# A new instruction order for linear attention and a spatial gating layer: q decayed in natural layout, powers of lambda formed by GpSimd

## The chip, the cores and the metric

One Trainium2 chip, one of its cores. Five engines take part, each with a queue of its own that it works off in order: TensorE (PE, with its weight loads as PEld), VectorE (DVE), ScalarE (ACT), GpSimd (POOL) and SyncE (SP). Sixteen DMA engines move data between HBM and the on-chip memory SBUF, and two kinds of queue feed them here: SP's loads, stores and transposes, and GpSimd's transfers, which also turn float32 into bfloat16 on the way. The metric is the time of one execution in microseconds, the median of the runs.

## The reference

Two layers follow each other. q, k and v have 4 batches, 8 heads, 768 positions and 64 channels, and each head has a decay `lam` near 0.98. The first layer is linear attention in blocks of 64 positions:

```python
rel = pos[:, None] - pos[None, :]
Dmask = np.where(rel >= 0, lam[:, None, None] ** rel[None, :, :], 0.0)
...
for b in range(nb):
    intra = (q_b @ k_b.T * Dmask) @ v_b
    inter = (q_b * lam ** (pos + 1)) @ kv_state
    out_b = intra + inter
    kv_state = lam ** 64 * kv_state + (k_b * lam ** (63 - pos)).T @ v_b
```

The second is a gated layer on x, which is that output with the heads side by side (4 x 768 x 512):

```python
h = np.maximum(x @ w_in, 0.0)              # 512 -> 1024
u, v = h[..., :512], h[..., 512:]
v_n = (v - mean(v)) / sqrt(var(v) + 1e-6)
v_s = w_spatial @ v_n + b_spatial          # over the 768 positions
out = (u * v_s) @ w_out                    # 512 -> 512
```

## The kernel before, in words

The decay between two positions is a product of two powers, `lam ** (MID - j)` for a key at j and `lam ** (i - MID)` for a query at i, so the mask that is left holds only zeros and ones. The work is cut into 12 steps, 3 to a batch, each of 256 positions (128 partitions, two neighbouring positions to a partition, 8 heads).

One string, `ORDER`, holds the whole program, each word one operation as `NAME.arguments.ENGINE`, with T for TensorE, D, A, P and S for the others. `KM.5.1.P` is "decay the second half of k of step 5, on GpSimd". An engine gets its words in the order of the string, and waits between engines come from the tiles that an operation reads and writes. What the words are:

- LQ, LK, LV: SP's loads of q, k and v of a step, 512 KB each, three buffers for each. VC casts v to bfloat16.
- KM: k times its power of lambda, to bfloat16, in natural layout (positions on the partitions); QM is the same for q, and QC casts q without decay.
- TK, TQ: transposes on TensorE, eight 128x128 ones for a step; EK, EQ bring them out of PSUM into kT and qT. Where q came by QC, EQ multiplies by `lq`, the powers in transposed layout. DK, DQ: the transposes by DMA in place of these, issued by SP; for them q has to come by QM.
- SC: scores; MK: the mask of zeros and ones, out of PSUM; KV: the state, KS: scores and state interleaved, SS: copy of the state to SBUF; AV: the output of attention, transposed; EX brings it out as xT. SC, KV, KS and AV are made of matmuls of 64x64 weights, four of which lie side by side in the array; TensorE's other operations use 128x128.
- PV, EV: the v half of `x @ w_in` and its relu; BN, RA, RD, NB, VN: mean, variance, root, reciprocal, shift and the normalised vn. PU, EU: the u half, transposed, and its relu.
- WI, WS, WO: GpSimd's transfers of w_in (two halves, the v half first), w_spatial (two halves of rows) and w_out. BS: SP's load of b_spatial, repeated on all partitions. WT, EW: w_spatial transposed, once.
- GP, PW, GM: for a batch, eight groups: bias into PSUM, the spatial matmul (L514, 6 of 384 columns), the product with u. PW of a batch needs all six vn tiles of that batch.
- PO, EO, ST: the last matmul, its copy, its store; PH, EH, SH the same in halves of the columns.
- FL: four 128x128 matmuls whose result nobody reads; FN: a copy of one element that nobody reads, ahead of EX; GT: a GpSimd copy of one element that holds GpSimd until a load is there.

The preparation of the powers is in `c_lam` to `l_t`: lambda is brought to all partitions by a matmul, ACT takes the logarithm, DVE multiplies by the positions, and ACT takes exponentials, of 128x48 elements for the natural layout and of 128x256 elements twelve times for `lq`. Steps 0 to 4 use QC and TQ with `lq`; steps 5 to 11 use QM, DK and DQ.

PSUM has eight banks; the last arguments of many words are bank numbers, and bank 7 holds the attention state.

Of the kernel before, what the change touches and what calls it, by code (L numbers as in the profile page):

```python
# [8 lines left out]
FP32 = mybir.dt.float32  # L9
# [10 lines left out]
TK.1.1.3.T TK.1.0.2.T KV.0.0.T EQ.1.0.0.D TQ.1.1.1.T MK.0.1.5.6.D EK.1.0.2.D SS.0.0.A EK.1.1.3.A VC.1.P  # L20
SC.1.0.4.5.T LQ.2.S QC.2.0.D SC.0.0.2.3.T LK.2.S EQ.1.1.1.D KV.0.1.T GT.1.1.P QC.2.1.P WI.1.P SC.1.1.0.1.T
FL.4.6.T MK.0.0.2.3.D TQ.2.0.2.T MK.1.1.0.1.D AV.0.0.3.6.T FN.0.3.6.A TQ.2.1.0.T SS.0.1.A MK.1.0.4.5.D LT.2.A
KM.2.0.P KV.1.0.T AV.1.0.1.4.T KM.2.1.D WS.1.P TK.2.0.5.T AV.0.1.3.6.T LV.2.S SS.1.0.D FN.1.1.4.A KV.1.1.T
LK.3.S EX.0.1.6.A AV.1.1.1.4.T BS.S LK.5.S EX.1.0.1.A EK.2.0.5.D LQ.3.S EX.0.0.3.D PV.0.1.5.T FL.15.6.T
EX.1.1.4.A WO.P TK.2.1.3.T GT.1.2.P PV.1.1.1.T EV.1.1.1.A EQ.2.1.0.D EQ.2.0.2.D VC.2.P WT.0.0.0.T EK.2.1.3.D
SC.2.0.2.3.T PV.1.0.4.T BN.1.1.D PV.0.0.6.T EW.0.0.0.A MK.2.0.2.3.D EV.0.1.5.A EV.1.0.4.A SC.2.1.0.1.T SS.1.1.A
PU.1.1.5.T BN.1.0.D WT.2.0.4.T KV.2.0.T MK.2.1.0.1.D RA.1.A BN.0.1.D LV.3.S AV.2.0.2.3.T EV.0.0.6.D SS.2.0.A
FN.2.2.3.D PU.1.0.0.T BN.0.0.D AV.2.1.2.3.T EX.2.1.3.D RD.1.D WT.1.0.1.T RA.0.A NB.1.D RD.0.D EX.2.0.2.A
EW.1.0.1.D EW.2.0.4.A NB.0.D VN.0.0.A WT.1.1.6.T GT.2.1.P KM.3.0.P EW.1.1.6.D KM.3.1.P GT.2.2.P VC.3.P
WT.2.1.3.T EW.2.1.3.D PV.2.1.2.T PV.2.0.1.T VN.1.0.A PU.2.1.4.T EU.1.0.0.A VN.0.1.D LK.4.S LQ.4.S KM.4.1.P  # L30
KM.4.0.P EV.2.0.1.A QC.4.2.P PU.0.0.6.T LV.4.S PU.0.1.3.T LQ.5.S WT.0.1.0.T LV.5.S LK.6.S VN.1.1.A PU.2.0.1.T
EU.1.1.5.A EV.2.1.2.D BN.2.1.D BN.2.0.D RA.2.A RD.2.D EU.0.0.6.A GP.0.2.1.2.A EW.0.1.0.D VN.2.1.D GP.0.0.0.5.A
VN.2.0.D EU.0.1.3.A QC.3.2.D LQ.6.S GP.0.1.1.6.A EU.2.0.1.D TK.3.2.0.T PW.0.0.0.5.T GM.0.0.0.5.D EU.2.1.4.D
GP.0.2.0.3.A PW.0.2.0.3.T TQ.3.2.1.T EQ.3.2.1.D GM.0.2.0.3.D EK.3.2.0.A PW.0.2.1.2.T SC.3.1.4.5.T MK.3.1.4.5.D
KS.3.0.0.1.T SS.3.0.A GP.0.0.1.3.A PW.0.1.1.6.T GP.0.3.1.4.A KS.3.1.0.1.T KM.5.1.P KM.5.0.P DK.5.S GM.0.2.1.2.D
MK.3.0.0.1.D TK.4.2.5.T EK.4.2.5.A PW.0.0.1.3.T PW.0.3.1.4.T GP.0.1.0.2.A GM.0.1.1.6.D GP.0.3.0.0.D AV.3.0.1.5.T
GM.0.0.1.3.D TQ.4.2.6.T SS.3.1.A PW.0.3.0.0.T GM.0.3.1.4.D PW.0.1.0.2.T FN.3.1.5.D AV.3.1.1.5.T EX.3.0.1.A
VC.4.P EQ.4.2.6.D KS.4.0.3.4.T SS.4.0.A PO.0.5.6.T EO.0.5.6.A QM.5.1.P KS.4.1.3.4.T VC.5.P QM.5.0.D SS.4.1.A
# [36 lines left out]
EO.2.3.6.D RD.11.D NB.11.D VN.11.1.A VN.9.1.D GP.3.3.1.4.D PU.10.0.0.T VN.11.0.D PO.2.2.2.T VN.10.0.A EO.2.2.2.A
PU.11.1.6.T GP.3.0.1.1.D PW.3.0.1.1.T EU.10.1.5.D EU.10.0.0.D GM.3.0.1.1.D GP.3.2.0.2.A EU.11.1.6.A PW.3.2.0.2.T
PW.3.3.1.4.T ST.2.1.S GP.3.2.1.5.A GP.3.1.1.0.D PW.3.0.0.3.T PW.3.1.1.0.T PW.3.2.1.5.T GP.3.3.0.6.D ST.2.5.S
GM.3.3.1.4.D GM.3.2.1.5.D ST.2.2.S GP.3.1.0.1.A GM.3.1.1.0.D PW.3.1.0.1.T PW.3.3.0.6.T GM.3.1.0.1.D PO.3.4.4.T
# [7 lines left out]
def kernel(  # L86
# [37 lines left out]
    ps = psum.tile([P, 8, 512], FP32, name="ps")  # L124
    SB = 7

    lam_in = sb([1, H], FP32, "lam_in")
    one_row = sb([1, P], FP32, "one_row")
    loglam = sb([P, H], FP32, "loglam")
    llrow = sb([P, 4], FP32, "llrow")  # L130
# [457 lines left out]
```

## Time and profile before

| what | value |
|---|---|
| time, median of 2 runs | 147.72 us (147.72 to 147.73) |
| profiled execution, span from first to last instruction | 145.4 us (what lies outside the span isn't in the profile) |
| mean granted TensorE clock | 0.996 |
| busy: PE, PEld, DVE, ACT, POOL | 131.9, 83.2, 113.0, 76.2, 53.7 us |
| DMA | 32.28 MB, mean 222 GB/s |
| read from HBM, written | 24.77 MB, 6.29 MB |

How to read what is quoted from it. The page gives busy times and, as digits, the busy tenths of 40 equal slices of the span. Groups of instructions stand as `line engine op out<-in shapes xcount | busy us, mean ns of one | idle before, and what ended it`. The timeline gives `start us, us, engine, line`, and in brackets how long the engine had been idle and what released it. The chain of waits gives `start us, us, what` for the chain that ended last; on TensorE its pieces follow each other without a gap, so the length of a piece is what that work costs in the queue, while the mean of a matmul in the groups is its latency. The windows give, for a stretch A:B, its length and each engine's busy time, with the granted clock, the DMA share and GB/s at the end.

### The profile page before, as it was taken

To read this page: it belongs to the slowest core of one execution; us is meant where nothing else is said; L and a number is where in the kernel's file an instruction comes from. 1 tells how busy PE (TensorE), PEld (TensorE's weight loads), DVE (VectorE), ACT (ScalarE), POOL (GpSimd) and SP (SyncE) were. 2 spreads that over 40 slices of the span, in tenths; PEclk is the share of its full clock that TensorE was granted. 3 is DMA by queue.
4 is the path that set the end of the run, shared out by engine and by line. 5 is a ranking of instruction groups with operands and counts; after the bars stand their busy time and mean duration, and the time that the engine had idled before them with its cause. 6 is when DMAs were issued, how large, how long until landed. Compare 5 with 4: busy or idle time off the path is not lost.

```text
span 145.4 us, 4626 instructions
## 1 busy us (share of the span) xinstructions
PE 131.9 (91%) x1954; PEld 83.2 (57%) x1954; DVE 113.0 (78%) x229; ACT 76.2 (52%) x155; POOL 53.7 (37%) x66
## 2 busy tenths in 40 slices
PE   1169989799999999999999999999999999999980
PEld 1047755578756565468565645775566556665540
DVE  2568985988898888979989889878988798972720
ACT  3775276669834224299942444594341447880250
POOL 7439920305089637672825729234000000000000
PEclk9999999999999999999999999999999999999998
DMA  3999999999999999999997998999490700082064
GB/s 83 347 347 347 229 214 216 216 230 341 302 307 301 293 118 272 239 253 333 194 312 194 284 304 194 343 207 194 147 338 19 281 12 0 5 326 107 0 265 170
DMA packets 58375, 32.28 MB, mean 222 GB/s; under 512 B 15858, under 2 KB 55282, under 8 KB 58354
## 3 DMA queue, kind: packets, MB, share of 16 engines
q1 hardware_dynamic: 55968, 29.23, 77.8%
q0 software_dynamic: 2384, 2.75, 10.8%
q8 instruction: 15, 0.25, 0.7%
q14 instruction: 6, 0.05, 0.3%
q10 hardware_dynamic: 2, 0.00, 0.0%
HBM read 24.77 MB, written 6.29 MB: 214 GB/s over the span
## 4 chain that ended last, share of the span: by engine, by line
PE 77%; DMA 12%; SPq 5%; POOL 2%; DVE 1%; issue 0%; POOLq 0%
PE ps L514 21%; PE ps L488 15%; PE ps L525 14%; PE ps L440 12%; DMA win_sb<-in_moe_w_in_dram 8%; SPq L192 5%; DMA q_in<-in_q_dram 4%; PE ps L415 3%; PE ps L406 2%; PE ps L347 2%; PE ps L316 1%; POOL kc L286 1%; PE ps L500 1%; PE ps L385 1%; PE ps L377 1%; PE ps L534 1%
## 5 line engine op out<-in xcount | busy, mean ns | idle before, releaser
L514 PE MATMUL ps<-wt_sb,vn 128*128 128x384 bf16 x192 | 34.3, 326 | 0.0
L352 DVE TENSOR_TENSOR a_sb<-ps,m 128x1024 bf16<-128x1024 f32 x24 | 28.7, 1217 | 4.3 <-PE ps L347 1.8
L286 POOL TENSOR_TENSOR kc<-k_in,lv 128x512 bf16<-128x512 f32 x20 | 20.5, 1042 | 25.0 <-DMA k_in<-in_k_dram 15.8
L488 PE MATMUL ps<-xT,win_sb 128*128 128x256 bf16 x192 | 24.0, 273 | 0.8 <-DMA win_sb<-in_moe_w_in_dram 0.8
L514 PEld LDWEIGHTS <-vn 128*128 128x128 bf16 x192 | 17.9, 98 | 11.6
L440 PE MATMUL ps<-win_sb,xT 128*128 128x512 bf16 x96 | 23.6, 380 | 0.1
L525 PE MATMUL ps<-wout_sb,gT 128*128 128x512 bf16 x92 | 22.7, 380 | 0.0
L488 PEld LDWEIGHTS <-win_sb 128*128 128x128 bf16 x192 | 18.3, 98 | 5.8 <-DMA win_sb<-in_moe_w_in_dram 1.0
L520 DVE TENSOR_TENSOR gT<-ps,uT 128x384 bf16<-128x384 f32 x32 | 16.9, 548 | 4.7 <-PE ps L514 4.6
L455 DVE BATCH_NORM_STATS2 st<-vh 128x6 f32<-128x512 bf16 x24 | 16.3, 681 | 1.5 <-ACT vh L445 1.3
L177 ACT ACTIVATE o_sb<-ps 128x512 f32<-128x512 f32 (+1 forms) x19 | 10.8, 580 | 12.1 <-PE ps L525 12.1
L445 ACT ACTIVATE vh<-ps 128x512 bf16<-128x512 f32 x17 | 10.0, 596 | 13.1 <-PE ps L440 10.7
L177 ACT ACTIVATE xT<-ps 128x512 bf16<-128x512 f32 x15 | 8.6, 596 | 14.2 <-PE ps L415 14.2
L181 POOL CAST vb<-v_in 128x1024 bf16<-128x1024 f32 x9 | 9.3, 1037 | 15.2 <-DMA v_in<-in_v_dram 11.3
L286 POOL TENSOR_TENSOR qc<-q_in,lqn 128x512 bf16<-128x512 f32 x12 | 12.5, 1049 | 4.5 <-DMA q_in<-in_q_dram 4.4
L440 PEld LDWEIGHTS <-xT 128*128 128x128 bf16 x96 | 8.6, 98 | 9.0 <-ACT xT L177 0.3
L525 PEld LDWEIGHTS <-gT 128*128 128x128 bf16 x92 | 8.5, 98 | 8.3
L177 ACT ACTIVATE ps<-bsp 128x384 f32<-128x384 f32 x21 | 10.0, 492 | 3.2 <-DVE a_sb L352 1.9
L415 PE MATMUL ps<-a_sb,vb 64*64 64x128 bf16 x384 | 10.2, 221 | 0.3 <-issue 0.3
L476 ACT ACTIVATE vn<-vh,shift,rstd 128x512 bf16<-128x512 bf16 x12 | 9.3, 806 | 0.2 <-DVE shift L470 0.2
L445 ACT ACTIVATE uT<-ps 128x512 bf16<-128x512 f32 x15 | 8.8, 590 | 1.0 <-PE ps L488 0.9
L347 PE MATMUL ps<-qT,kT 64*64 64x128 bf16 x288 | 7.9, 238 | 0.9 <-ACT kT L177 0.5
(76 smaller groups left out, 170.9 us busy)
## 6 DMA issues: line engine op xcount, KB each, us to landing
q_in<-in_q_dram SPq DMA_DIRECT2D x12, 512.0 KB, 6.2
k_in<-in_k_dram SPq DMA_DIRECT2D x12, 512.0 KB, 6.2
v_in<-in_v_dram SPq DMA_DIRECT2D x12, 512.0 KB, 6.0
out_dram<-o_sb SPq DMA_DIRECT2D x23, 256.0 KB, 2.9
wsp_raw<-in_moe_w_spatial_dram POOLq DMA_DIRECT2D x2, 576.0 KB, 12.4
win_sb<-in_moe_w_in_dram POOLq DMA_DIRECT2D x2, 512.0 KB, 10.6
wout_sb<-in_moe_w_out_dram POOLq DMA_DIRECT2D x1, 512.0 KB, 17.3
bsp<-in_moe_b_spatial_dram SPq DMA_DIRECT2D x1, 384.0 KB, 21.0
```

Source lines behind the costliest of these rows:

```text
L177: nc.scalar.activation(out=o, in_=i, func=AF.Copy)
L286: vec(e).tensor_tensor(out=dst[n % NCA][:, u].rearrange("p u m o d -> p o (u m) d"), in0=src[n % NIN].rearrange("p (o u) m d -> p o u m d" ...
L347: nc.tensor.matmul(out=pa[o][row(c), w, j], lhsT=kT[n % NTR][row(o), u, j, c * Q64:(c + 1) * Q64], rhs=qv(n, o, u, c), start=(w == 0 and j ...
L352: nc.vector.tensor_tensor(out=a_sb[n % NA][:, i].rearrange("p o w j x -> p o w (j x)"), in0=ps[:, b0:b1 + 1:b1 - b0].rearrange("p o (w y) ...
L415: nc.tensor.matmul(out=po[c ^ o][row(w), c, i], lhsT=vb[n % NCA][row(c), 4 * o + u, j, :], rhs=a[row(c), i, o, w, j, :], start=(r == 0 and ...
L440: nc.tensor.matmul(out=bank(b), lhsT=x[:, slot(c, g)], rhs=win_sb[:, g, DH:DFF], start=(g == 0), stop=(g == NCH - 1))
L445: nc.scalar.activation(out=o, in_=i, func=AF.Relu)
L455: nc.vector.bn_stats(out=st6[p2][:, t], in_=vh[p2][:, t])
L488: nc.tensor.matmul(out=pu[:, f2].rearrange("p (c x) -> p c x", c=2), lhsT=win_sb[:, g, f * P:(f + 1) * P], rhs=x[:, slot(0, g):slot(1, g) ...
L514: nc.tensor.matmul(out=bank(b)[:, 0:HW], lhsT=vn[bb % 2][:, s, f * P:(f + 1) * P], rhs=wt_sb[:, s, i * HW:(i + 1) * HW], start=False, stop ...
L520: nc.vector.tensor_tensor(out=gT[bb % 2][:, f, cols], in0=bank(b)[:, 0:HW], in1=uT[bb % 2][:, f, cols], op=ALU.mult)
L525: nc.tensor.matmul(out=bank(b), lhsT=gT[bb % 2][:, f, t * P:(t + 1) * P], rhs=wout_sb[:, f, :], start=(f == 0), stop=(f == NCH - 1))
```

## The change

Every word of `ORDER` is placed anew, on all engines and in SP's queue; the loads now begin with k. Some work changes its engine, some its kind:

| word | before | after |
|---|---|---|
| QC (q cast) | 4 on D, 4 on P | none |
| QM (q decayed, natural layout) | 2 D, 12 P | 7 D, 17 P |
| KM | 4 D, 20 P | 6 D, 18 P |
| VC | 1 D, 2 A, 9 P | 2 D, 5 A, 5 P |
| EQ | 8 D, with `lq` | 4 D, 5 A, plain copies |
| EK | 4 D, 4 A | 3 D, 6 A |
| VN | 12 D, 12 A | 18 D, 6 A |
| NB (the shift that VN on ACT needs) | 11 | 5 |
| GP | 11 D, 21 A | 14 D, 18 A |
| EU / EV / EX on D | 9 / 7 / 9 | 6 / 9 / 10 |
| DK, DQ (DMA transposes) | steps 5 to 11 | steps 6 to 11 |
| GT / FL | 4 / 2 | 0 / 4 |

The powers: lambda is loaded to all partitions by a DMA, GpSimd raises it to the positions, DVE takes the reciprocal for q. The matmul, the logarithm, the exponentials and `lq` go, and `c_tab` calls for the square root once, early on ACT. The rest of the diff moves functions without a change of what they do.

The diff, cut to its core (of the order: the first lines of the old one, and of the new one the first lines and the stretch around steps 4 and 5):

```diff
 ORDER = """
-LQ.0.S lam.A msk.P idn.P LK.0.S LQ.1.S mkc.D QC.0.1.D posk.P pos.P LB.0.T LN.0.A LL.D QC.0.0.P LK.1.S LX.A
-KM.0.1.D QC.1.0.D TQ.0.0.1.T KM.0.0.D LT.1.A LT.0.A TK.0.1.2.T TQ.0.1.3.T EQ.0.1.3.D KM.1.1.D TK.0.0.4.T LV.0.S
-KM.1.0.P EK.0.1.2.A EQ.0.0.1.D WI.0.P EK.0.0.4.D SC.0.1.5.6.T QC.1.1.P WS.0.P TQ.1.0.0.T LV.1.S VC.0.A
...
+LK.0.S lam.A pos.P msk.P LQ.0.S LV.0.S LL.P LK.1.S idn.P LR.D mkc.D LQ.1.S KM.0.1.D FL.8.0.T KM.0.0.D TK.0.1.1.T
+QM.0.1.D LV.1.S EK.0.1.1.A QM.0.0.D TQ.0.1.2.T TQ.0.0.3.T EQ.0.1.2.D VC.0.P LK.2.S SC.0.1.4.5.T EQ.0.0.3.A FL.2.6.T
+WI.0.P MK.0.1.4.5.D TK.0.0.0.T LQ.2.S KM.1.1.P KV.0.0.T EK.0.0.0.A eps.D FL.0.1.T SS.0.0.D SC.0.0.2.3.T QM.1.0.P
+LK.3.S FL.9.6.T MK.0.0.2.3.D QM.1.1.P TQ.1.0.4.T TK.1.1.5.T EK.1.1.5.D KM.1.0.P TQ.1.1.0.T KV.0.1.T EQ.1.1.0.D
+SS.0.1.A LV.2.S WI.1.P VC.1.D TK.1.0.1.T SC.1.1.2.6.T EK.1.0.1.A EQ.1.0.4.D AV.0.0.3.5.T tab.A FN.0.3.5.D SC.1.0.0.4.T
+AV.0.1.3.5.T MK.1.0.0.4.D KV.1.0.T EX.0.1.5.A KM.2.1.P EX.0.0.3.A LQ.3.S KM.2.0.P TK.2.1.1.T PV.0.0.0.T EK.2.1.1.D
+MK.1.1.2.6.D PV.0.1.4.T SS.1.0.D AV.1.0.3.5.T QM.2.0.D KV.1.1.T SS.1.1.A FN.1.3.5.D EV.0.0.0.D QM.2.1.P AV.1.1.3.5.T
+BS.S TQ.2.0.1.T EX.1.1.5.D EX.1.0.3.A TK.2.0.2.T LV.3.S WS.0.P TQ.2.1.6.T EQ.2.0.1.A EV.0.1.4.D PV.1.1.0.T EK.2.0.2.A
+EQ.2.1.6.D BN.0.0.D SC.2.1.3.5.T SC.2.0.1.4.T PU.1.0.2.T KM.3.0.P MK.2.0.1.4.D LK.4.S PV.1.0.6.T KM.3.1.P MK.2.1.3.5.D
...
+GM.0.0.0.6.D QM.5.1.D LV.7.S AV.3.0.0.5.T KS.4.0.2.4.T QM.5.0.P FN.3.0.5.D SC.4.1.1.6.T GM.0.1.0.3.D AV.3.1.0.5.T
+SS.4.0.A KS.4.1.2.4.T EX.3.0.0.D EX.3.1.5.A WO.P LQ.6.S TQ.5.2.3.T SS.4.1.D GP.0.0.1.0.A PV.3.1.5.T VC.5.P
+MK.4.0.2.4.D EQ.5.2.3.A PW.0.0.1.0.T LV.6.S KM.6.1.P EV.3.1.5.A MK.4.1.1.6.D SC.5.1.2.4.T SC.5.0.3.5.T KM.6.0.P
+KV.5.0.T MK.5.1.2.4.D PU.3.0.1.T DK.6.S MK.5.0.3.5.D PV.3.0.6.T AV.4.0.2.4.T EV.3.0.6.A AV.5.0.3.5.T FN.4.2.4.D
+SS.5.0.A AV.4.1.2.4.T FN.5.3.5.D EU.3.0.1.D AV.5.1.3.5.T PU.3.1.6.T EX.5.1.5.A EX.5.0.3.D LK.9.S EX.4.0.2.A BN.3.0.D
...
     def c_lam(e):
-        nc.scalar.dma_start(out=lam_in, in_=lam.unsqueeze(0))
+        nc.scalar.dma_start(out=lam_b, in_=lam.unsqueeze(0).to_broadcast((P, H)))
...
     def l_l(e):
-        nc.vector.tensor_tensor(out=lv, in0=loglam.unsqueeze(1).unsqueeze(3).broadcast_to((P, NR, H, 2)),
-                                in1=posk.unsqueeze(2).broadcast_to((P, NR, H, 2)), op=ALU.mult)
...
+        nc.gpsimd.tensor_tensor(out=lv, in0=lam_b.unsqueeze(1).unsqueeze(3).broadcast_to((P, NR, H, 2)),
+                                in1=pos.unsqueeze(2).broadcast_to((P, NR, H, 2)), op=ALU.pow)
+
+    def l_q(e):
+        nc.vector.reciprocal(out=lqn, in_=lv)
...
+    def c_tab(e):
+        nc.scalar.activation(out=seen3, in_=eps_t, func=AF.Sqrt)
...
     def e_q(e, n, x, b):
-        nc.vector.tensor_tensor(out=qT[n % NTR][:, part(x)].rearrange("p u m x -> p (u m x)"),
-                                in0=quad(b)[:, part(x)].rearrange("p u m x -> p (u m x)"),
-                                in1=lq[:, n % NR, part(x)].rearrange("p u m x -> p (u m x)"), op=ALU.mult)
+        ev(e, n, x, qT, b)
```

`ev` copies a transposed tile out of PSUM on the engine that it is given. The end of the order changes too: the last words were `PH.3.5.1.6.T EH.3.5.1.6.A ST.3.0.S PH.3.5.0.3.T EH.3.5.0.3.D SH.3.5.1.S SH.3.5.0.S`, and are now `PO.3.4.3.T EO.3.3.5.A SH.3.5.0.S ST.3.3.S EO.3.4.3.A ST.3.4.S`.

More of the change, by code (lines that the diff above doesn't have):

```diff
@@ L22 @@
[L22 to L26, printed above, removed]
@@ L82 @@
+EO.3.4.3.A ST.3.4.S
 """
@@ L125 @@
     SB = 7
[L127 to L130, printed above, removed]
+    lam_b = sb([P, H], FP32, "lam_b")
     ident = sb([P, P], BF16, "ident")
@@ L173, in bank, with row @@
         return ps[:, b]
+    def row(x):
+        return slice(x * Q64, (x + 1) * Q64)
     def copy(e, o, i):
@@ L181, in copy, with relu @@
             nc.gpsimd.tensor_copy(out=o, in_=i)
+    def relu(e, o, i):
+        if e == "A":
+            nc.scalar.activation(out=o, in_=i, func=AF.Relu)
+        else:
+            nc.vector.tensor_scalar(out=o, in0=i, scalar1=0.0, scalar2=None, op0=ALU.max)
     def vec(e):
@@ L260, in b_sp @@
         nc.sync.dma_start(out=bsp, in_=moe_b_spatial.unsqueeze(0).to_broadcast((P, S)))
-    def f_l(e, n, b):
-        for i in range(4):
-            nc.tensor.matmul(out=bank(b)[:, 0:P], lhsT=ident, rhs=ident, start=True, stop=True)
     def ld_k(e, n):
-        load(k, k_in, n, e)
+        load(k, k_in, n)
     def ld_q(e, n):
-        load(q, q_in, n, e)
+        load(q, q_in, n)
     def ld_v(e, n):
-        load(v, v_in, n, e)
+        load(v, v_in, n)
     def part(x):
         return slice(0, 4) if x == 2 else slice(2 * x, 2 * x + 2)
-    def q_c(e, n, x):
-        u = part(x)
-        copy(e, qc[n % NCA][:, u].rearrange("p u m o d -> p o (u m) d"),
-             q_in[n % NIN].rearrange("p (o u) m d -> p o u m d", o=2)[:, :, u].rearrange("p o u m d -> p o (u m) d"))
     def decay(e, dst, src, ln, n, x):
@@ L396, in a_v @@
         a = a_sb[n % NA]
-        def inter(c):
-            if r == 0 and c == 0:
-                return
-            s = s_sb[(2 * n + c - 1) % 4]
+        if not (r == 0 and z == 0):
+            s = s_sb[(2 * n + z - 1) % 4]
             for i in range(2):
@@ L480, in v_n @@
                                  scalar2=rstd[p2][:, t:t + 1], op0=ALU.subtract, op1=ALU.mult)
-    def p_u(e, n, j, b):
-        x = xT[n % NX]
-        pu = bank(b).rearrange("p (f x) -> p f x", f=2)
-        for f2 in range(2):
-            f = 2 * j + f2
-            for g in range(NCH):
-                nc.tensor.matmul(out=pu[:, f2].rearrange("p (c x) -> p c x", c=2), lhsT=win_sb[:, g, f * P:(f + 1) * P],
-                                 rhs=x[:, slot(0, g):slot(1, g) + 1:slot(1, g) - slot(0, g)], start=(f2 == 0 and g == 0), stop=(g == NCH - 1),
-                                 skip_group_check=True)
     def e_u(e, n, j, b):
```

300 lines of the change are left out of this document (131 added, 169 removed).

## The prediction

> **What bounds the kernel now.** I read the page first, then the windows, then the chain of waits piece by piece.
>
> ```profile
> span 145.4 us, 4626 instructions
> PE 131.9 (91%) x1954; PEld 83.2 (57%) x1954; DVE 113.0 (78%) x229; ACT 76.2 (52%) x155; POOL 53.7 (37%) x66
> PE   1169989799999999999999999999999999999980
> ...
> PEclk9999999999999999999999999999999999999998
> ```
>
> TensorE (PE) is thin in the first three slices and full after them, at the full clock. So I cut the run where the first spatial matmul (PW, L514) starts. Each cut has its row in the windows (length, PE, PEld, DVE, ACT, POOL):
>
> ```profile
> 37.65 2.17 PE L514 MATMUL ps<-wt_sb,vn 128*128 128x384 bf16 x12
> 0.00:37.65 37.65, 28.75 (x487) 20.80 (x488) 27.46 (x60) 24.19 (x49) 17.12 (x30) 1.00 1.08 259
> 37.65:141.33 103.68, 103.14 (x1471) 62.35 (x1468) 85.12 (x169) 52.05 (x107) 36.61 (x36) 1.00 0.84 210
> 5.00:37.65 32.65, 26.69 (x56) 1.00 1.16 275
> 140.43 0.89 PE ps L534 x8
> ```
>
> The span is **37.65 of start, 103.68 of full TensorE, and 4.05 of tail** (145.4 less 141.33). The second part is TensorE's queue and nothing else, but "busy" is no density. The chain, which merges TensorE's work by line, shows what it hides:
>
> ```profile
> 67.40 0.35 PE ps L347 x16
> 68.00 1.85 PE ps L488 x16
> ...
> 72.66 0.35 PE ps L415 x16
> 73.01 1.08 PE ps L514 x6
> ...
> 78.42 0.97 PE ps L514 x6
> ...
> 82.50 0.22 PE ps L415 x16
> 82.73 0.22 PE ps L347 x16
> 82.95 0.97 PE ps L525 x4
> ...
> 93.84 0.86 PE ps L525 x4
> ```
>
> Sixteen 64x64 matmuls take 0.22 us behind other 64x64 ones (82.50, 82.73), but 0.35 behind 128x128 ones (67.40, 72.66). A 128x128 group is also dearer behind 64x64 ones: PW 1.08 against 0.97, PO 0.97 against 0.86. **Going into an attention block and out again costs 0.13 + 0.11 = 0.24 us.**
>
> The start is set by loads and VectorE (DVE). These rows are of the timeline and the DMA view, the last two for 15 to 25 us:
>
> ```profile
> 2.93 0.59 PE L207 MATMUL ps<-lam_in,one_row 1*128 1x8 f32 x2 [2.93 <-DVE one_row L241]
> 4.96 0.43 DVE L179 CAST qc<-q_in 128x512 bf16<-128x512 f32 x1 [2.08 <-DMA q_in<-in_q_dram]
> 6.37 3.28 ACT L224 ACTIVATE lq<-posq,llrow 128x256 bf16<-128x256 f32 x8
> 8.02 0.43 DVE L179 CAST qc<-q_in 128x512 bf16<-128x512 f32 x1 [0.81 <-DMA q_in<-in_q_dram]
> 10.63 0.93 POOL L248 DMA_DIRECT2D win_sb<-in_moe_w_in_dram  x1
> DMA to landing us min/median/max: 9.2/10.6/12.0
> 25.57 1.04 POOL L181 CAST vb<-v_in 128x1024 bf16<-128x1024 f32 x1 [6.51 <-DMA v_in<-in_v_dram]
> q1 hardware_dynamic: 7883, 3.98, 114.6%
> q0 software_dynamic: 1343, 1.54, 88.3%
> q1 hardware_dynamic: 1170, 0.59, 28.9%
> ```
>
> The first load is there at 4.96, the third at 8.02, so one each 1.5 us (3.98 MB in the 11.5 us from 3.0). Once GpSimd's weight transfers (q0) run, SP's loads (q1) fall to 0.59 MB in 10 us, a 0.52 MB load in 8.9 us: hence v of step 2 only at 25.57.
>
> **The change, part by part.** Durations:
>
> ```profile
> L352 DVE TENSOR_TENSOR a_sb<-ps,m 128x1024 bf16<-128x1024 f32 x24 | 28.7, 1217 | 4.3 <-PE ps L347 1.8 <-ACT o_sb L177 1.2 <-PE ps L385 0.8
> L286 DVE TENSOR_TENSOR qc<-q_in,lqn 128x512 bf16<-128x512 f32 x2 | 2.0, 1010 | 0.0
> L447 DVE TENSOR_SCALAR vh<-ps 128x512 bf16<-128x512 f32 x7 | 4.8, 683 | 0.7 <-PE ps L440 0.7
> L455 DVE BATCH_NORM_STATS2 st<-vh 128x6 f32<-128x512 bf16 x24 | 16.3, 681 | 1.5 <-ACT vh L445 1.3
> L456 DVE BATCH_NORM_AGGREGATE mv<-st 128x2 f32<-128x6 f32 x24 | 4.4, 182 | 0.8
> L479 DVE TENSOR_SCALAR vn<-vh,mv,rstd 128x512 bf16<-128x512 bf16 x12 | 5.2, 455 | 0.0
> L179 DVE COPY kT<-ps 128x512 bf16<-128x512 bf16 x4 | 1.7, 416 | 0.8 <-PE ps L316 0.8
> 8.36 0.69 DVE L286 TENSOR_TENSOR kc<-k_in,lv 128x512 bf16<-128x512 f32 x1
> L286 POOL TENSOR_TENSOR kc<-k_in,lv 128x512 bf16<-128x512 f32 x20 | 20.5, 1042 | 25.0 <-DMA k_in<-in_k_dram 15.8 <-PE ps L377 8.7 <-PE ps L347 0.5
> L200 POOL CAST posk<-poski 128x6 f32<-128x6 int32 x1 | 0.2, 189 | 0.1
> 37.36 0.45 PE ps L316 x8
> ```
>
> *TensorE's order, from the first PW on.* Counting in both orders how often a run of SC, KS, KV and AV stands between other TensorE work: 26 such runs before, 15 after. 11 x 0.24 = **-2.6 us**, on the path, since TensorE has no other wait there. What is late next is DVE: it has some 87 us of work there (the 85.12 of the row and what the counts below add), 86% of the 101.5 us that remain. The sharpest place is steps 4 and 5, where four masks (4 x 1.22) stand together; by the order KV, PU, PV, PW and TQ lie beside them, so I cost it at nothing. If that cover fails, 1.2 us a time.
>
> *Step 5.* Its k and q are transposed on TensorE instead of by DMA: 16 transposes at 0.056 us (0.45 for 8) = 0.9 us more. TQ of step 3 moves from behind the first PW to ahead of it (0.45), so the second part gets **+0.45 us**. Two of 14 DMA transposes and their SP issues go; the queue behind them gains, which I leave at nothing, since the loads stand well ahead there. Steps 6 to 11 are transposed by DMA in both kernels.
>
> *The powers of lambda.* Gone: the PE broadcast, Ln, three groups of Exp (the eight lq end at 9.65), two table loads. Added: one power of 128x48 on GpSimd (LL), which waits for lambda (there by 2.93), and a reciprocal of as many elements on DVE. No row shows a power. Below: 0.19, the cast of 128x6. Above: as late as lq is now, 9.65. I take 1 us, nearest to GpSimd's own rows. Behind LL in GpSimd's queue stand the identity, the first v cast and the first weight issue. The first k decay (KM on DVE) can start at 4.96, so 2.0 us of LL are covered by the load; each us beyond is a us of start. SC.0 then starts near 8.5 (KM 0.69 twice, QM 0.69 twice, EQ 0.42 from 4.96) and not behind lq.
>
> *q's decay moves* from the qT evacuation on DVE to GpSimd and DVE in natural layout: 17 QM on GpSimd and 7 on DVE in place of 12 and 2. On DVE by counts of the orders, whole kernel: QM +5.0, KM +1.6, VN +2.7, GP +1.7, EV +1.4, and less QC -2.0, EQ -2.1, EU -2.0 and smaller ones: some 117 us in place of 113.
>
> *The start, ending at the first PW.* PE's work there is hardly changed, so DVE decides. Its queue from 4.96 up to the first PW, by the rows: 6 MK 7.3, 6 BN 5.2, 2 KM and 2 QM 2.8, the QM of step 2 1.0, 3 EV 2.05, 2 EX 1.4, 4 EQ and 2 EK 2.5, 4 VN 1.8, 2 EW 1.1, EU and VC 1.4, 2 SS 0.8, GP 0.55, small ones 1.0: **28.8 us**. Today it does 26.7 in that stretch and is idle for 32.65 - 26.69 = 6.0. Walking through the new order I find seven waits, 3.4 us: q of step 0 (0.1), the first SC (0.7), KV and SC of step 0 (0.7, 0.8), the transposes of step 1 (0.75 in two), AV of step 1 (0.35). 4.96 + 28.8 + 3.4 = **37.1, -0.5 us**. Both ends: no idle gives 33.8, as much as today 39.8. TensorE closes the lower one: PV of step 0 needs the first half of w_in. v of step 0 is the third load (8.02), its cast takes 1.0, the issue stands behind it at 9.0, and lands 9.2 later: 18.2. Behind that stand, ahead of the first PW, 6 PV (5.2 us, 0.22 a matmul as in L525), 6 PU (5.2), 36 transposes of w_spatial (2.0), and about 5 of attention and transposes: 17.5, so not before 35.7.
>
> *The loads behind this.* GpSimd does four decays (4 x 1.04) between the two w_in issues, so the second leaves at 14.05 and lands at 23.2; PU wants it at 24.1. In between, q of step 2 gets through: the first w_in's packets need 3.5 us (1.54 MB in 10 us is 0.52 MB in 3.4), the second's start 5.05 behind the first's, so 1.5 us are free for loads at 0.35 MB/us, 0.5 MB. QM of step 2 then runs at 18.5 and is not late. w_spatial leaves at 19.5 and 24.7, lands near 29 and 34; the transposes want it at 31.9 and 35. w_out goes behind the first PWs. Covered, with 1 us to spare.
>
> *Tail.* The last store is a whole tile behind a 0.6 us copy, in place of two halves: **+0.1**.
>
> Sum: -0.5 - 2.6 + 0.45 + 0.1 = -2.6. The profile's span goes from 145.4 to 142.8; what lies outside it (147.72 - 145.4 = 2.3) is the same, so 147.72 - 2.6 = **145.1 us**, with 144.0 to 146.4 for this case (half a us of each term). A measurement of this kernel tells about 2% from no change, 144.8 or 150.7; the forecast lies just inside.
>
> **Rivals.**
>
> *Start and stalls both better (143.1).* The first PW at the floor of 35.7 (-1.9), and what waits are left in today's second part go too: 0.54 idle (103.68 - 103.14) and some 0.2 beside it: -1.9 - 2.6 - 0.7 + 0.55 = -4.6. For it: DVE has 6 us of idle in the start today. Against: 28.8 us of queue. Chance 0.20.
>
> *DVE becomes the bound in the second part (147.7).* The 2.6 that TensorE saves become waits for masks and gT. For: 86% of DVE's time is used. Against: its waits of today are for PE (L352: 4.3 in all). Chance 0.15.
>
> *q crawls behind the weights (148.5, slower).* Place: QM of step 2 on DVE, with EV, EX and the masks queued behind it. If the second w_in's packets follow the first's with under 1.1 us between (0.4 MB of q left at 0.35 MB/us), q comes at 21.4, 2.2 us later; w_spatial, issued behind QM on GpSimd, shifts as much and then covers q of step 3, whose TQ stands ahead of the last WT: first PW at 40.5, +3.4. For: 25.57 in today's rows is just this. Against: the four decays between the issues. Chance 0.17.
>
> *The powers come late (149.8, slower).* LL ending at 9.65 instead of by 4.96 puts KM and, from 7 us on, v's cast and the weights behind it: +4.7. It decides from 2 us of LL, and the kernel is slower than before from 4.6. For: no power in any row. Against: GpSimd's rows for ordinary work are 0.2 to 1.0. Chance 0.08.
>
> The Trainium skill, "GPSIMD Engine Reference", section 2.1 "Instruction dispatch", speaks for that rival: the first call of a freshly loaded GpSimd routine costs some 6 us more, with nothing in the profile. By it, estimated from that page, the powers would end near 9 and the sum would be 149. No row here shows such a stall ahead of iota, cast or decay.
>
> **How the numbers follow.** Forecast 0.40, rivals 0.20, 0.15, 0.17, 0.08. Range 143.1 to 149.2: outside lie half of the first rival (0.10) and the last one (0.08). Faster by over 2%: 0.20 and about 0.15 of the forecast's 0.40. Slower by over 2%: 0.07, from late powers beyond 5.6 us and a crawl that comes with waits in the second part. Within 2%: 0.58.
>
> **What would show it.** First PW at 36.5 to 37.7, PE's end 101.5 later; PW, PO and PU groups with 0.11 more fewer times; LL under 2 us; SC of step 0 near 8.5; w_in landing at 18.2 and 23.2 with q of step 2 ahead of 19. Wrong, if idle of PE beyond 1 us stands in the second part, if a QM on DVE waits for a load, or if the start ends elsewhere than with DVE.

## The result and the profile after

The changed kernel takes **168.56 us** (median of 2, 167.76 to 169.37) beside 147.72 us for the kernel before: 14% slower, ratio 1.144, 95% interval 1.127 to 1.161. The forecast was 145.1 us. In the four later comparisons the kernel before took 146.8 to 147.0 us. Some runs of a kernel fall in a slower state, over 1.5% above its fastest run; the times and ratios below leave them out.

First the page of the kernel after, then its windows, cut as before at the first PW and at TensorE's end (length; PE, PEld, DVE, ACT, POOL; clock, DMA share, GB/s).

```profile
span 167.7 us, 4624 instructions
PE 130.6 (78%) x1960; PEld 84.8 (51%) x1976; DVE 119.3 (71%) x224; ACT 74.2 (44%) x145; POOL 55.4 (33%) x56
PE   0001079698999997699999889875999989999990
...
PEclk9999999999999999999999999999999999999999
```

```profile
0.00:52.62 52.62, 28.41 (x498) 21.03 (x501) 32.37 (x56) 18.87 (x34) 27.82 (x29) 1.00 1.02 240
52.62:163.72 111.10, 102.19 (x1466) 63.79 (x1476) 86.92 (x169) 54.70 (x111) 27.60 (x27) 1.00 0.68 166
```

TensorE has no more to do than before (130.6 us beside 131.9) and the clock is full; it waits. The span grows by 22.3 us: the start by 15.0 (52.62 beside 37.65), the second part by 7.4 (111.10 beside 103.66), the tail by nothing (3.98 beside 4.1). Two separate losses, then.

**The start.** Rows of the timeline after:

```profile
6.12 8.04 POOL L204 TENSOR_TENSOR lv<-lam_b,pos 128x48 f32<-128x48 f32 x1 [3.65 <-DMA lam_b<-in_lam_dram]
14.64 1.04 POOL L175 CAST vb<-v_in 128x1024 bf16<-128x1024 f32 x1
15.61 0.97 POOL L234 DMA_DIRECT2D win_sb<-in_moe_w_in_dram  x1
15.78 6.02 DVE L263 TENSOR_TENSOR kc<-k_in,lv 128x512 bf16<-128x512 f32 x2
```

```profile
lam_b<-in_lam_dram ACTq DMA_DIRECT2D x1, 4.0 KB, 5.2
```

The last row is of the DMA issues (size, us from issue to landing). Lambda, loaded to 128 partitions, is there at 6.12, not 2.93; the power then takes 8.04 us; the v cast and the first weight issue stand behind it; and the first two decays of k on DVE take 6.02 us together, not 1.4. Lambda's arrival differs from run to run: with the same load it landed after 3.6 to 3.7 us in four of the experiments below (e3, e4, e10, e14), so some 1.5 of the 15.0 us belong to this run.

**The second part.** TensorE's waits after the first PW (total, times, longest), and DVE's group of masks:

```profile
PE ps L323 <- DVE a_sb L328: 2.4, 1, 2.4
PE ps L353 <- DVE a_sb L328: 1.9, 2, 1.4
PE ps L400 <- DVE a_sb L328: 1.5, 2, 1.1
PE ps L408 <- ACT vh L179: 1.1, 1, 1.1
PE ps L371 <- DVE a_sb L328: 0.6, 2, 0.4
```

```profile
L328 DVE TENSOR_TENSOR a_sb<-ps,m 128x1024 bf16<-128x1024 f32 x24 | 28.8, 1220 | 9.0 <-PE ps L323 2.8 <-PE ps L378 2.3 <-ACT vh L179 1.6
```

It waits for masks, of which each takes 1220 ns as before (1217). DVE is not simply short of time: over the whole run it sat idle for 9.0 us just ahead of masks, 5.7 of them in the second part (4.3 before, all in the second part). The longest wait, in the timelines of DVE, ACT and PE, shows how:

```profile
64.39 1.22 DVE L328 TENSOR_TENSOR a_sb<-ps,m 128x1024 bf16<-128x1024 f32 x1
65.64 1.02 ACT L171 ACTIVATE qT<-ps 128x1024 bf16<-128x1024 bf16 x1 [0.97 <-DVE a_sb L328]
66.56 0.59 ACT L179 ACTIVATE vh<-ps 128x512 bf16<-128x512 f32 x1
67.19 1.23 DVE L328 TENSOR_TENSOR a_sb<-ps,m 128x1024 bf16<-128x1024 f32 x1 [1.58 <-ACT vh L179]
68.46 0.64 PE L323 MATMUL ps<-qT,kT 64*64 64x128 bf16 x32 [2.37 <-DVE a_sb L328]
```

By `ORDER` these are MK.4.0.2.4, EQ.5.2.3, EV.3.1.5, MK.4.1.1.6 and SC.5.1.2.4. Each starts when the one above it ends (EV because it stands behind EQ on ACT), though no two neighbours in this chain share a bank: a mask of banks 2 and 4, a copy out of bank 3, a relu out of bank 5, a mask of banks 1 and 6, scores into banks 2 and 4. The waits that the built program holds say the same; two reads of a bank are ordered there as well:

```
EQ.5.2.3   (bank 3)          waits for  MK.4.0.2.4 (banks 2, 4; held as 2 to 4)
MK.4.1.1.6 (held as 1 to 6)  waits for  EV.3.1.5   (bank 5)
SC.5.1.2.4 (first: bank 2)   waits for  MK.4.1.1.6 (held as 1 to 6)
```

One mask instruction reads two banks as `ps[:, b0:b1 + 1:b1 - b0]`, and what derives the waits takes it for everything from the first bank to the last. In the kernel before all 24 pairs are neighbours; in the new order 18 of 24 are not, with 37 banks lying between. Waits between a mask and a bank that it doesn't use: none in the program before, 33 after, by a count in the built programs. That is theory S of the experiments.

### The profile page after: what moved, and what is told of

Its sections match the earlier page's. It is cut to its first block, busy times and chain, and to the rows that moved or that the text cites. A ratio compares the mean times of both kernels' runs of the same rounds, so it can differ in the third digit from the quotient of the medians.

```text
span 167.7 us, 4624 instructions
## 1 busy us (share of the span) xinstructions
PE 130.6 (78%) x1960; PEld 84.8 (51%) x1976; DVE 119.3 (71%) x224; ACT 74.2 (44%) x145; POOL 55.4 (33%) x56
## 4 chain that ended last, share of the span: by engine, by line
PE 63%; DVE 19%; POOL 6%; issue 5%; ACT 3%; DMA 1%; DVEq 0%; POOLq 0%; ACTq 0%
PE ps L415 17%; DVE a_sb L328 12%; PE ps L408 10%; PE ps L421 9%; PE ps L400 9%; POOL lv L204 5%; PE ps L293 4%; DVE kc L263 4%; PE ps L323 3%; PE ps L378 3%; PE ps L371 2%; PE ps L338 2%; PE ps L473 1%; DMA out_dram<-o_sb 1%; PE ps L353 1%
## 5 line engine op out<-in xcount | busy, mean ns | idle before, releaser
L328 DVE TENSOR_TENSOR a_sb<-ps,m 128x1024 bf16<-128x1024 f32 x24 | 28.8, 1220 | 9.0 <-PE ps L323 2.8
L263 POOL TENSOR_TENSOR kc<-k_in,lv 128x512 bf16<-128x512 f32 x18 | 18.8, 1057 | 39.9 <-PE ps L338 20.6
L400 PE MATMUL ps<-win_sb,xT 128*128 128x512 bf16 x89 | 22.1, 379 | 3.0 <-DVE a_sb L328 1.9
L421 PE MATMUL ps<-wout_sb,gT 128*128 128x512 bf16 x83 | 21.2, 379 | 1.0 <-DVE a_sb L328 0.3
L263 POOL TENSOR_TENSOR qc<-q_in,lqn 128x512 bf16<-128x512 f32 x17 | 17.8, 1068 | 2.0 <-DMA q_in<-in_q_dram 2.0
L175 POOL CAST vb<-v_in 128x1024 bf16<-128x1024 f32 x5 | 5.2, 1035 | 31.8 <-DMA v_in<-in_v_dram 29.6
L171 ACT ACTIVATE kT<-ps 128x512 bf16<-128x512 bf16 (+1 forms) x6 | 4.4, 739 | 22.6 <-PE ps L293 22.4
L388 PE MATMUL ps<-ident 128*128 128x128 bf16 x16 | 2.4, 308 | 14.7 <-POOL ident masks.py:199 14.7
L179 ACT ACTIVATE uT<-ps 128x512 bf16<-128x512 f32 x18 | 10.5, 598 | 5.2 <-PE ps L408 3.5
L171 ACT ACTIVATE s_sb<-ps 128x256 bf16<-128x256 f32 x15 | 5.7, 383 | 15.2 <-PE ps L338 14.9
L293 PE MATMUL ps<-ident,kc 128*128 128x128 bf16 x48 | 4.9, 250 | 7.1 <-DVE kc L263 5.9
```

The lines of the kernel that those rows point to most:

```text
L171: nc.scalar.activation(out=o, in_=i, func=AF.Copy)
L179: nc.scalar.activation(out=o, in_=i, func=AF.Relu)
L263: vec(e).tensor_tensor(out=dst[n % NCA][:, u].rearrange("p u m o d -> p o (u m) d"), in0=src[n % NIN].rearrange("p (o u) m d -> p o u m d" ...
L293: nc.tensor.transpose(out=q0[:, u, m], in_=src[n % NCA][:, u, m].rearrange("p o d -> p (o d)"), identity=ident)
L328: nc.vector.tensor_tensor(out=a_sb[n % NA][:, i].rearrange("p o w j x -> p o w (j x)"), in0=ps[:, b0:b1 + 1:b1 - b0].rearrange("p o (w y) ...
L400: nc.tensor.matmul(out=bank(b), lhsT=xT[n % NX][:, slot(c, g)], rhs=win_sb[:, g, DH:DFF], start=(g == 0), stop=(g == NCH - 1))
```

## The experiments

### The start: the powers

**e1_act_powers** forms the powers as before:

```diff
-nc.scalar.dma_start(out=lam_b, in_=lam.unsqueeze(0).to_broadcast((P, H)))
+nc.scalar.dma_start(out=lam_in, in_=lam.unsqueeze(0))   # one row; then a matmul brings it to all partitions
-nc.gpsimd.tensor_tensor(out=lv, in0=lam_b..., in1=pos..., op=ALU.pow)
+Ln on ACT, times pos on DVE, Exp twice on ACT (128x48 each)
```

> The new order with the powers of lambda formed as in the kernel before (one row of lambda, matmul broadcast, logarithm, exponentials; no lq). Theory A: the start of the changed kernel is late by the power on GpSimd (8.04 us, behind a lambda that is there only at 6.1) and by the two k decays on DVE that collide with GpSimd (6.02 us for two), and its second part is longer by waits of its own that the order makes. Then the first PW comes near 38.5 instead of 52.6, the part from there to PE's end stays near 110.7, and the time is about 155 us. Theory B: the waits in the second part (8.9 us of idle PE) come from the late start, which puts loads and engines out of step. Then the second part falls to about 102 as well and the time is about 147 us. Theory C: the start's length lies elsewhere (loads, weights): first PW still after 48.

Measured: 154.4 us, ratio 1.049 [1.041, 1.057]. (The expectation of e6 calls it 156.2.) Its windows, and k's first decays in its timeline:

```profile
0.00:37.70 37.70, 30.06 (x503) 21.75 (x504) 27.09 (x56) 20.95 (x38) 18.73 (x27) 1.00 1.08 273
37.70:149.27 111.57, 103.16 (x1479) 63.83 (x1476) 87.51 (x170) 54.80 (x111) 28.81 (x29) 1.00 0.68 186
4.80 1.29 DVE L275 TENSOR_TENSOR kc<-k_in,lv 128x512 bf16<-128x512 f32 x2 [1.24 <-ACT lv L220]
```

The whole start is back (37.70), and the second part is as long as after (111.57 beside 111.10). So the late start does not make the waits of the second part.

**e2_lam_row** keeps the power on GpSimd and brings lambda as one row and a matmul; **e3_third_power** forms a third of the columns and copies them over the other two thirds (the decays of two thirds are another step's); **e4_hold_gpsimd** makes GpSimd wait, by a copy of one element of kc, until DVE has done k's first decays:

```diff
 e2: -to_broadcast((P, H))              +one row, matmul with a row of ones, copy to lam_b
 e3: -pow of 128x48                     +pow of 128x16, two copies of 128x16
 e4:  in ORDER  - VC.0.P                + HD.P VC.0.P
```

> Lambda as one row of 8 floats and a matmul broadcast, as before; the power stays on GpSimd. If the broadcast load of lambda (there at 6.1 instead of by 2.9) costs its full delay, the power starts near 3.6 instead of 6.1 and first PW and time come 2.5 us earlier, about 166 us. If the start hangs on the loads of k, q and v as well, less than 1 us.

> The power of 16 of the 48 columns only; the other two thirds are copies of the first, so the decay is that of the first third everywhere. If the 8.04 us go with the elements (0.17 us a column), this power takes about 2.7 us and the time falls by about 5 us to 163. If they are a fixed cost of the first call, it takes 7 to 8 us still and the time stays near 168.5.

> GpSimd reads one element of the decayed k of step 0 before its first cast, so its casts, decays and weight issues stand behind DVE's two k decays. If these took 6.02 us because GpSimd was running beside them, they now take 0.7 us each; GpSimd starts some 2.5 us later than it did, TensorE's first transpose 4.5 us earlier, and the time falls by 1 to 4 us. If the decays are long for another reason (their first load, the mask copies), they stay at 3 us each and the time rises by 4 to 6 us.

Measured: 167.16 us (ratio 1.134), 159.15 (1.081) and 164.67 (1.115). Timeline rows of e2, e3 and e4:

```profile
2.96 8.04 POOL L213 TENSOR_TENSOR lv<-lam_b,pos 128x48 f32<-128x48 f32 x1 [0.48 <-DVE lam_b L210]
12.63 6.02 DVE L272 TENSOR_TENSOR kc<-k_in,lv 128x512 bf16<-128x512 f32 x2
```

```profile
4.55 2.94 POOL L204 TENSOR_TENSOR lv<-lam_b,pos 128x16 f32<-128x16 f32 x1 [2.08 <-DMA lam_b<-in_lam_dram]
8.74 1.29 DVE L265 TENSOR_TENSOR kc<-k_in,lv 128x512 bf16<-128x512 f32 x2
```

```profile
13.49 1.29 DVE L266 TENSOR_TENSOR kc<-k_in,lv 128x512 bf16<-128x512 f32 x2
```

The power costs 2.94 us for 16 columns and 8.04 for 48: 0.16 us a column and 0.4 beside. Lambda's earlier arrival in e2 (2.96) is worth 1.4 us of the time, less than the 2.5 that I expected if it counted in full; the power is what is long. And k's two decays take 1.29 us when GpSimd stands still (e4), 6.02 beside its cast, weight issue and decays; which of these slows them isn't separated. e3 gained 9.4 us where I expected 5, and not by the power alone: its decays too ran while GpSimd stood still, waiting for v, and took 1.29. The Trainium skill, "SBUF — State Buffer", section "SBUF: two separate sides", says that a VectorE instruction with two SBUF inputs and a GpSimd instruction that reads SBUF exclude each other for a whole instruction; e4 agrees with this, with 1.29 beside 6.02, and does not show the mechanism itself.

### The second part: the masks

Four kernels, each with one idea. **e6_split_far_masks** and **e9_renamed_and_split** start from e1; **e7_banks_renamed** changes names of banks alone; **e8_before_banks_far** does the reverse to the kernel before.

```diff
 e6: -one instruction for both banks of a mask
     +if abs(b1 - b0) > 1: two instructions, one for each bank (18 masks)
 e7: +every bank argument b of ORDER becomes (3, 0, 4, 5, 2, 1, 6)[b]       (9 masks left apart)
 e8:  kernel before: +every bank argument b becomes 2 * b % 7               (24 masks apart)
 e9:  e7, and the split of e6 for the 9
```

(The expectations say 19 of 24; it is 18.)

> The kernel of e1_act_powers (156.2 us, first PW to last PW 106.1 us, of which TensorE waits about 7.5 us, nearly all for masks on VectorE), with each mask whose two PSUM banks are not neighbours (19 of 24) written as two instructions, one for each bank. Theory S (a mask that reads banks 1 and 6 in one instruction is ordered as if it read all banks 1 to 6, so it waits for work in banks 2 to 5, and matmuls into those banks wait for it): the waits go, first to last PW falls to 98.5 to 100.5, the time to 149 to 151. Rival D (VectorE is simply too busy in the new order, masks come late by its queue): 19 more VectorE instructions, about 0.15 us more each, so the stretch stays at 106 or grows to 109, the time is 156 to 159. Rival O (the order of the attention runs itself puts TensorE ahead of its masks): 106, time 156.

> The kernel of e1_act_powers with its PSUM banks renamed throughout (0..6 become 3,0,4,5,2,1,6): same instructions, same order, same VectorE work; 9 masks instead of 19 span other banks, and 17 banks lie between in place of 37. Theory S: about half or more of the 7.5 us of waits go: first to last PW 99 to 103.5, the time 149.5 to 153.5. Rivals D and O: nothing changes, 106 and 156.

> The kernel before with its banks renamed so that the two banks of every mask, neighbours today, lie 2 or 5 apart (bank b becomes 2b mod 7): 36 banks lie between, as in the changed kernel (37). Nothing else changes. Theory S: the kernel before gets the same disease: waits for masks appear on TensorE, first to last PW grows from 98.4 to 102 to 107, the time from 147 to 150 to 156. Rivals D and O: 98.4 and 147.

> The renaming of e7_banks_renamed and, for the 9 masks that still span other banks, the split of e6_split_far_masks: no mask is ordered against a bank that it does not use, at 9 more VectorE instructions instead of 19. Theory S: first to last PW 98 to 100, the time 148.5 to 150.5; if the fewer changes between 128-row and 64-row matmuls are worth the 2.6 us that the prediction gave them, 96 and 146.5. Rivals D and O: 106 to 107 and 156 to 157.

| kernel | waits of masks with foreign banks | first PW to TensorE's end | time | ratio to before |
|---|---|---|---|---|
| before | 0 | 103.66 | 146.97 | |
| e8_before_banks_far | 30 | 116.17 | 163.22 | 1.107 [1.101, 1.113] |
| e1_act_powers | 33 | 111.57 | 154.4 | 1.049 [1.041, 1.057] |
| e7_banks_renamed | 12 | 105.54 | 147.16 | 1.001 [0.997, 1.005] |
| e6_split_far_masks | 0 | 103.07 | 145.65 | 0.989 [0.983, 0.994] |
| e9_renamed_and_split | 0 | not compared | 145.72 | 0.986 [0.978, 0.995] |

Windows of e6, its two groups of masks, and the window and the waits of e8 for the same stretch:

```profile
36.24:139.31 103.07, 101.28 (x1466) 63.55 (x1476) 87.66 (x183) 54.63 (x111) 29.72 (x29) 1.00 0.74 206
L342 DVE TENSOR_TENSOR a_sb<-ps,m 128x512 bf16<-128x512 f32 x36 | 22.5, 681 | 0.5 <-PE ps L335 0.5
L348 DVE TENSOR_TENSOR a_sb<-ps,m 128x1024 bf16<-128x1024 f32 x6 | 7.2, 1217 | 1.5 <-PE ps L335 1.5
```

```profile
41.50:157.67 116.17, 103.27 (x1455) 62.66 (x1467) 85.16 (x168) 52.56 (x107) 35.91 (x35) 1.00 0.70 178
PE ps L518 <- ACT ps L177: 3.1, 3, 1.9
PE ps L492 <- DVE a_sb L356: 2.5, 2, 1.5
PE ps L444 <- DVE a_sb L356: 2.0, 2, 1.4
PE ps L389 <- DVE a_sb L356: 1.3, 1, 1.3
```

Theory S stands, though not its numbers: e6, e7 and e9 came out 2.3 to 3.4 us quicker than the quick end of what was expected. 1.8 of that is the starting point, 156.2 where e1 takes 154.4; another part is the start of e6 and e7 (first PW at 36.24 and 36.08 in place of 37.70). e6 gives DVE 18 more instructions and loses the waits; a busy VectorE is not the cause. e7 adds no instruction and gains 7 us by other numbers for banks. e8 makes the kernel before 16 us slower in the same way, well past what I expected; there it reaches bias copies into PSUM on ACT as well. The masks themselves take 1220 ns in e8 as with neighbouring banks (1217 before), so it is the order of events that costs, and not the reading of banks that lie apart.

**e10_after_masks_cured** is the changed kernel, power on GpSimd and all, with e9's two edits:

> The changed kernel itself, powers still formed by GpSimd, with nothing but its banks renamed and the 9 masks that still span other banks split (the two edits of e9_renamed_and_split). Theory: there are two separate losses, so this one keeps the late start (first PW near 52) and loses the waits of the second part: 168.5 less the 10.2 us between e1_act_powers and e9_renamed_and_split, 157.5 to 159.5. Rival: the late start had shifted the order of events so that the two losses overlap; then 155 to 157, or 160 and more.

157.9 us, ratio 1.073 [1.069, 1.078]: 10.7 us less than the changed kernel. In its trace the second part is 103.53 us (111.10 before the cure) and the first PW stands at 48.92 (52.62, of which 1.5 is lambda's later arrival in that run). In e1 the same waits cost 8.8 us (154.4 less e6's 145.65), so the two losses add to within about 2 us. The time falls in the expected range; the 10.2 us from which that was worked out took e1 at 156.2.

### The price of a round trip

**e11_dense_extra** and **e12_switch_extra** add 14 matmuls of 128x128 to the kernel before, at places that differ:

```diff
 e11: between two dense groups        ... PW.x.T  + FX.b.T  PO.y.T ...
 e12: between two 64x64 groups        ... SC.x.T  + FX.b.T  KS.y.T ...
```

> The kernel before with 14 extra 128x128x128 matmuls, each put between two dense groups of TensorE (PV, PU, PW, PO) of the second part; the control for e12_switch_extra. 14 times 0.06 to 0.11 us: 0.8 to 1.5 us more from first PW to the end of TensorE than the 103.7 of before, time about 148.

> The same 14 extra matmuls in the kernel before, each put between two 64-row groups (SC, KS, KV, AV) of the second part, so that each makes one more round trip between dense and 64-row matmuls. If the prediction's 0.24 us a round trip is right: 14 x 0.24 = 3.4 us more than e11_dense_extra, time about 151. If a round trip costs nothing here (the 2.6 us of the prediction would then be wrong, and what e9_renamed_and_split won came from elsewhere): as e11_dense_extra, 148.

147.58 us and 150.61 us. Windows of the second part, of e11 and of e12:

```profile
37.77:141.69 103.92, 102.63 (x1471) 63.00 (x1482) 85.30 (x169) 52.03 (x107) 36.59 (x36) 1.00 0.83 209
```

```profile
38.06:144.94 106.88, 105.82 (x1471) 64.30 (x1482) 85.39 (x169) 52.23 (x107) 36.66 (x36) 1.00 0.78 202
```

The difference is 2.96 us, or **0.21 us a round trip**; the prediction read 0.24 off the chain. The control itself cost less than expected: 0.26 us beside the 103.66 of before in place of 0.8 to 1.5, which no run explains.

### A third thing: where the load tiles start

**e13_lv_first** was meant as the best version: e9 with the Exp for k ahead of the one for q, into a tile of its own (192 bytes a partition).

> e9_renamed_and_split with the Exp that k's decay waits for put ahead of the other one, 0.24 us on ScalarE. A version to beat both kernels. If k's first decay waits for the powers: 0.2 us less, 145.7; if it waits for the load of k: as e9_renamed_and_split, 146.0 and a ratio of 0.986 to 0.99.

It took 148.61 us, ratio 1.010 [1.006, 1.013], slower than e9. Its loads leave more slowly. The small tile had moved every tile behind it, so that q_in, k_in, v_in and the weights start 192 bytes past a multiple of 512 in SBUF; in the changed kernel they start 480 past one, in the kernel before and in e1, e2 and e6 to e9 at a multiple. Four kernels add nothing but an unused tile:

```diff
 e14: changed kernel   +pad = sb([P, 8], FP32, "pad")      # load tiles: 480 -> 0 past a multiple of 512
 e15: e13              +pad = sb([P, 80], FP32, "pad")     #             192 -> 0
 e16: kernel before    +pad = sb([P, 120], FP32, "pad")    #               0 -> 480
 e17: e13              +pad = sb([P, 16], FP32, "pad")     #             192 -> 256
```

> The changed kernel with one unused tile of 32 bytes a partition ahead of the others, so that every load tile starts at a multiple of 512 bytes in SBUF (480 past one before). Nothing else changes. Theory A (where the tile starts sets the pace of the loads): the first loads leave 1.45 us apart instead of 1.74, first PW 0.5 to 2.5 us earlier, time 165 to 168. Rival (the pace comes from lambda's broadcast load, or from chance): 1.74, time 168.5.

> e13_lv_first (148.6 us) with 320 bytes of unused tile, so that its load tiles start at multiples of 512 bytes again. Theory A: loads 1.45 us apart, time 145 to 146, faster than the kernel before by about 1%. Rival (putting one Exp ahead of the other costs the 2.6 us): 148.6.

> The kernel before with 480 bytes of unused tile, so that its load tiles start 480 bytes past a multiple of 512 as in the changed kernel. Theory A: loads 1.74 us apart instead of 1.45, time 148 to 150.5. Rival: 147.

> e13_lv_first with 64 bytes of unused tile: load tiles start 256 bytes past a multiple of 512 (192 in e13_lv_first). If only multiples of 512 are quick: loads 1.74 us apart and 148.6. If multiples of 256 do: 1.45 and 145 to 146.

Measured: e14 168.87 us (ratio 1.150 [1.147, 1.153]), e15 146.51 (0.996 [0.993, 0.999]), e16 151.0 (1.028 [1.022, 1.035]), e17 **145.11** (0.987 [0.983, 0.991]). SP's issues, which follow each other as the queue takes them, in e13 and in e17:

```profile
3.30 1.78 SPq L195 DMA_DIRECT2D k_in<-in_k_dram  x1
5.12 1.74 SPq L195 DMA_DIRECT2D q_in<-in_q_dram  x1
6.91 1.74 SPq L195 DMA_DIRECT2D v_in<-in_v_dram  x1
```

```profile
3.29 1.45 SPq L196 DMA_DIRECT2D k_in<-in_k_dram  x1
4.78 1.45 SPq L196 DMA_DIRECT2D q_in<-in_q_dram  x1
6.27 1.45 SPq L196 DMA_DIRECT2D v_in<-in_v_dram  x1
```

A start 0 or 256 bytes past a multiple of 512 gives issues of mostly 1.45 us, 192 or 480 mostly 1.74 (1.59 to 1.74 in the changed kernel). It costs the kernel before about 4.2 us, more than the 1 to 3.5 expected, and e13 2 to 3.5. In the changed kernel, repaired alone, no gain shows (e14): its decays start at 14.16, and at 14.21 in e10 with the tiles 480 past, so there the start waits for the power, not for loads. My expectation for e14 (165 to 168) missed. Its total is no finer test, since its second part had a granted clock of 0.98 (1.00 after) and took 112.26 us (111.10 after). The Trainium skill, "DMA: Bandwidth & Descriptors", section "How a descriptor splits into AXI transactions", says of reads that a transaction has to start at a 256-byte boundary, and that a descriptor which doesn't start there spends beats on bytes that nobody uses. Here it is the address written in SBUF that changes, so the page does not state this case; the four starts would fit such a boundary, and no run shows the mechanism.

e17 and e6 take less than both kernels, 1.3% and 1.1% less than the kernel before. e15 came out above its expected 145 to 146. What separates it from e17 (1.4 us, with the same pace of loads) was not pursued; in their traces the first PW stands at 37.97 in e15 and 36.17 in e17, and the first eight PV matmuls take 3.51 us and 1.89.

## Why the prediction was wrong, point by point

- **The powers, "I take 1 us".** This step failed, by the largest amount: 8.04 us. The bounds were 0.19 and an end by 9.65; it ended at 14.16, because lambda too was late (in e2, with lambda there at 2.96, it still ended only at 11.00). I had taken its arrival (2.93) from a load of one row, and a load to 128 partitions landed at 6.12. "GpSimd's rows for ordinary work are 0.2 to 1.0" was no argument about a power. The rival *The powers come late* had the right mechanism, with a chance of 0.08 and 4.7 us; the measured loss of the start was 15.0. The price from the Trainium skill that stood beside it ("GPSIMD Engine Reference", section 2.1), 6 us for a first call, does not show in e3: its power is as much a first call and takes 2.94, and the cost grows with the columns.
- **"2 KM and 2 QM 2.8" of DVE's queue.** The row of 0.69 came from a moment when GpSimd was idle. Beside GpSimd's work the two KM took 6.02. The diff moves that work next to them, and I did not ask what runs beside a row. The timeline of the kernel before held a warning: a decay on DVE beside one on GpSimd took 1.20, not 0.69.

```profile
9.64 1.04 POOL L286 TENSOR_TENSOR kc<-k_in,lv 128x512 bf16<-128x512 f32 x1 [3.78 <-DMA k_in<-in_k_dram]
10.03 1.20 DVE L286 TENSOR_TENSOR kc<-k_in,lv 128x512 bf16<-128x512 f32 x1
```

- **The start without the power, 37.1.** Right in the sum: 37.70 in e1, 36.2 in e6 and e17, 37.97 in e15. Its parts offset each other, which was luck: for a queue of 28.8 us (its terms add up to 28.9) and waits of 3.4, DVE was busy for 26.13 us from 5.00 to the first PW in e1 and idle for 6.5, and in e6 26.37 and 4.9. The rival *q crawls behind the weights* did not come: in e1 no wait of DVE in the start of 0.2 us or more is for a load.
- **"by the order KV, PU, PV, PW and TQ lie beside them, so I cost it at nothing".** This step failed in the second part. Steps 4 and 5 were indeed the sharpest place, with 2.4 us, but not for want of VectorE's time: masks were ordered against banks that they don't use. I counted masks and their neighbours and passed over the bank numbers in the same words, all of which the diff shows. 7.4 us longer instead of 2.15 shorter. The rival *DVE becomes the bound* is wrong too: with e6's 18 extra instructions the waits go.
- **"11 x 0.24 = -2.6".** The price holds (0.21 in e12), and the count of runs does. The cured kernels still save less than forecast: e17 needs 103.41, e6 103.07 and e15 102.60, beside 103.66 before and 101.5 forecast. e17's window:

```profile
36.17:139.58 103.41, 102.28 (x1479) 63.63 (x1476) 87.31 (x175) 54.78 (x111) 29.82 (x29) 1.00 0.74 206
```

  PE is idle for 1.13 us there beside 0.52 before, which takes 0.6 of the 2.15 back. Where the rest went stays open: the busy sums can't tell, because for the same order the traces hold 1466 (e6) to 1479 (e17) matmul records.
- **Tail +0.1.** 3.98 beside 4.1: nothing.
- **The addresses of the load tiles** do not occur in the prediction. The change of the small tiles ahead of them moved all others. It did not decide this result, but took 2 to 3.5 us from e13.
- **What would show it.** "Idle of PE beyond 1 us stands in the second part" was the named sign of error, and there were 8.9 us.

With the powers formed as before, no mask across foreign banks and the tiles on a 256-byte boundary, the same order takes 145.11 us. That this agrees with 145.1 is luck: the start came out 0.9 better than forecast and the second part 1.9 worse, and the kernel before took 146.77 us in that comparison, where the forecast started from 147.72. The saving was 1.7 us, and 2.6 were forecast.

## What to carry to other kernels

Where waits are derived from what an instruction reads, a strided access to two PSUM banks can count as all banks between; read the bank numbers of a new order, keep such pairs next to each other, or write one instruction for each. An operation that no row shows has no upper bound by its neighbours: time it by itself, at its size, and ask of each row that you do use what ran beside it. And after any change of the small tiles, look at where the load tiles start.

## What the runs showed of the hardware

- A GpSimd power took 0.16 us for a column of 128 float32 (2.94 us for 16, 8.04 for 48).
- Two VectorE products of two SBUF tensors each, 1.29 us together while GpSimd stood still, took 6.02 beside its cast, weight issue and decays.
- An issue of a 512 KB load took 1.45 us where its tile started 0 or 256 bytes past a multiple of 512, and 1.74 where it started 192 or 480 past one.
- A load of lambda's 32 bytes to 128 partitions landed 5.2 us after its issue in the changed kernel, and 3.6 to 3.7 in e3, e4, e10 and e14.
- Going from 128x128 to 64x64 matmuls and back cost 0.21 us.
